# Opening of a fused attention and soft-mixture kernel: four token tiles with two heads on alternate partitions, loads on two queues

## The chip, the core and the metric

The kernel runs on one core of a Trainium2 chip. TensorE (PE) multiplies into PSUM, VectorE (DVE), ScalarE (ACT) and GpSimd (POOL) work beside it, SyncE (SP) issues loads and stores, and the DMA engines move them. The metric is device microseconds (us) of one execution; lower is better.

## The reference

Three stages follow each other. All is float32, except the first mixture's weights, which come as float64 and are narrowed on the chip.

```
# attention by chunks of 32 tokens; 4 batches, 8 heads, 768 tokens, 64 wide
q_c = q[:, :, c_start:c_end]
k_full = concat([mem_k, k[:, :, l_start:r_end]])   # 8 memory + 16 + 32 + 8 keys
a = softmax(scale * q_c @ k_full.T);  out[:, :, c_start:c_end] = a @ v_full
# a rational network on x = [3072 tokens, 512]
h = x @ w_in                                        # 2048 wide
g = (a0 + a1*h + a2*h*h + a3*h*h*h) / (1 + |b0|*|h| + |b1|*h*h + 1e-6)
x = g @ w_out
# soft mixture of 8 experts with 4 slots each
logits = x @ phi;  d = softmax(logits, over tokens);  c = softmax(logits, over slots)
slot_out[e] = relu((d.T @ x)[e] @ w1[e]) @ w2[e];  return c @ slot_out
```

## The kernel before

The 3072 tokens are six blocks of 512. A block has four tiles of 128 tokens, or two **pairs** of tiles. For a pair, `attention` multiplies queries and keys (line L168, scores), takes the largest score of each row (L186), subtracts it (L189), takes exponentials (L190), turns the result on PE so that keys lie on partitions (L208, copied out by ACT in L212), sums (L197 to L199), multiplies with the values (L228, here called **PV**), scales (L238), turns the token rows (L246) and copies them into `xt`, the block's x with features on partitions (L250). Two heads share a tensor: one has partitions 0 to 63, the other 64 to 127, and each L168 or L228 multiplies one head, one chunk of 32 tokens, over 64 partitions, so that a pair takes 64 matmuls for the scores and 64 for PV.

Then a block has eight **steps** of 256 hidden columns: `h_part` (L380, eight float32 matmuls of 512 columns in block 0, none of whose x or weights is split), ACT's Abs, Square and Identity of h (L610, L611, L613), DVE's denominator (L612) and numerator (L622, L623), ACT's Ln and Exp (L627, L628) for the reciprocal, POOL's product (L588) and two more on DVE (L635, L636). Block 0 also narrows each step's weights from float64: `f64_narrow` is a scaled copy on ACT (L303), a clamp on DVE (L304), a Prelu on ACT (L305) and a shift with or on DVE (L307). The pieces of w_in are called i0 to i7, those of the transposed w_out o0 to o7. All through block 0 the pairs of block 1 are attended to in slices between the steps.

The **opening** is what stands ahead of the first step: pair 0 (tiles A and B of the block) and pair 1 (tiles C and D), i0 to i2 narrowed, and h of step 0. Its order on PE, ACT, DVE and POOL is written out by hand: the string `pre` names generators, of which each letter advances one to its next yield (`fN` issues N dummy matmuls, L288). `loads` gives the loads in order; SP issues them all, in its own queue. Behind the opening a scheduler orders the engines from the sequence of the code (`ord0` for block 0). Each engine works through its own order strictly; SP too. Loads use eight semaphores in turn, so a load is issued only when the one eight places ahead has landed. The pools of buffers rotate: `p_g` has four (a staging buffer of 1 MB each for one i or o), `p_xt` four, `p_x` two, `ps_h` two buffers of PSUM.

Of the kernel before, what the change touches and what calls it, by code (L numbers as in the profile page):

```python
# [46 lines left out]
def tile_chunk_attention__rational__soft_moe(  # L47
# [103 lines left out]
    def attention(pair, tile4=None, after=None):  # L151
        tile4 = tile4 or (lambda shape: p_a4("a4", shape))
        after = pair + 1 if after is None else after
# [3 lines left out]
        if pair < 2:  # L157
            both = ps_h("h", [P, 2, 2, HP, WIN])
            sc = [both[:, par] for par in range(2)]
        else:  # L160
            sc = [bank([P, 2, HP, WIN]) for _ in range(2)]
# [56 lines left out]
        if pair < 2:
            both = ps_h("h", [P, 2, 2, HP, D])
            pv = [both[:, par] for par in range(2)]  # L220
        else:
            pv = [bank([P, 2, HP, D]) for _ in range(2)]
# [718 lines left out]
```

## Time and profile before

| | us |
|---|---|
| median of three runs (574.03 to 574.85) | 574.24 |
| the profiled execution, its own time | 573.23 |
| its span in the trace | 571.1 |
| PE busy | 537.9 (94%) |
| DVE busy | 455.7 (80%) |
| ACT busy | 427.8 (75%) |
| POOL busy | 122.8 (21%) |

The span is what the trace covers; 2.1 us of the profiled execution lie around it. The shares are means over stages with different limits. TensorE's granted clock is 0.984 of full speed over the span. The trace shows each float32 matmul of the attention and of block 0 as two rows, a transpose as one; "64*32 64x64" is a stationary tile of 64 partitions by 32 columns and an output of 64 columns.

### The profile page before, as it was taken

The numbers are of one execution on the slowest core, as the hardware profiler recorded it, in microseconds if no ns is written. First come the engines' busy times: TensorE is split into PE (matmuls) and PEld (weight loads), VectorE is DVE, ScalarE is ACT, GpSimd is POOL, SyncE is SP. The second block draws the span as 40 slices with busy tenths as digits, with TensorE's granted clock in tenths as the row PEclk, the third lists the DMA queues.
The fourth block names the chain that finished last, engine by engine and source line by source line (L and its number), as shares of the span: only waits on it lengthen the run. The fifth ranks groups of instructions, "written<-read, shape, count | busy, mean of one in ns | idle before, by whom it ended". The sixth has DMA issues, their size and how long they took to land.

```text
span 571.1 us, 13640 instructions
## 1 busy us (share of the span) xinstructions
PE 537.9 (94%) x5874; PEld 360.2 (63%) x5874; DVE 455.7 (80%) x572; ACT 427.8 (75%) x551; POOL 122.8 (21%) x66
## 2 busy tenths in 40 slices
PE   6799899999999999999999999999999999999981
PEld 5654445467667677677766777776778667643351
DVE  4749999999989899979799799897898978831041
ACT  1669999998978899688887887878888978721132
POOL 0001111422213132313222213132323332300000
PEclk9699999999999999999999999999999999999997
DMA  8897763313225223533233315313359264799948
GB/s 322 352 393 268 259 223 117 116 64 113 63 86 185 76 80 143 185 112 94 93 112 111 133 57 183 112 48 138 111 178 376 94 239 147 293 397 409 408 163 355
DMA packets 28139, 105.80 MB, mean 185 GB/s; under 512 B 3376, under 2 KB 3504, under 8 KB 27056
## 3 DMA queue, kind: packets, MB, share of 16 engines
q1 hardware_dynamic: 26928, 100.74, 48.4%
q0 software_dynamic: 1152, 4.19, 1.8%
q8 instruction: 46, 0.75, 0.5%
q14 instruction: 13, 0.11, 0.1%
HBM read 94.44 MB, written 10.49 MB: 184 GB/s over the span
## 4 chain that ended last, share of the span: by engine, by line
PE 47%; DVE 25%; ACT 12%; DMA 7%; issue 6%; POOL 1%; SPq 1%; ACTq 0%; DVEq 0%; POOLq 0%
PE h L380 24%; PE m L405 4%; DMA win<-in_moe_w_dram 3%; DVE T L623 3%; PE lg L398 3%; DVE T L622 3%; PE m L458 3%; DVE S L612 3%; ACT S L610 3%; DVE T L635 3%; ACT S L611 2%; DVE T L636 2%; PE m L228 2%; DVE g L304 2%; DMA T<-in_moe_w_dram 2%
## 5 line engine op out<-in xcount | busy, mean ns | idle before, releaser
L380 PE MATMUL h<-xt,win 128*128 128x512 f32 x1012 | 266.8, 412 | 1.5 <-DVE T L623 1.3
L380 PEld LDWEIGHTS h<-xt,win 128*128 128x128 f32 x1012 | 183.7, 188 | 51.0 <-issue 12.3
L588 POOL TENSOR_TENSOR S<-S,S 128x1024 f32<-128x1024 f32 x46 | 112.8, 2452 | 329.5 <-DVE S L612 329.5
L610 ACT ACTIVATE S<-h,ctab 128x1024 f32<-128x1024 f32 x47 | 52.5, 1117 | 40.3 <-PE h L380 39.5
L612 DVE SCALAR_TENSOR_TENSOR S<-S,S 128x1024 f32<-128x1024 f32 x47 | 57.3, 1218 | 28.4 <-ACT S L611 28.2
L405 PEld LDWEIGHTS m<-ident,T 128*128 128x128 f32 x384 | 43.0, 141 | 30.7 <-issue 16.2
L622 DVE TENSOR_TENSOR T<-T,h 128x1024 f32<-128x1024 f32 x47 | 56.9, 1210 | 6.2 <-ACT T L613 6.2
L623 DVE SCALAR_TENSOR_TENSOR T<-T,ctab,h 128x1024 f32<-128x1024 f32 x47 | 59.8, 1271 | 0.7
L635 DVE SCALAR_TENSOR_TENSOR T<-T,ctab,S 128x1024 f32<-128x1024 f32 x46 | 58.6, 1274 | 0.0
L406 ACT ACTIVATE g<-m 128x512 f32<-128x512 f32 x96 | 53.5, 602 | 6.5 <-PE m L405 6.3
L636 DVE SCALAR_TENSOR_TENSOR T<-S,T 128x1024 f32<-128x1024 f32 x46 | 56.1, 1220 | 2.0
L613 ACT ACTIVATE T<-h,ctab 128x1024 f32<-128x1024 f32 x47 | 57.4, 1221 | 0.0
L405 PE MATMUL m<-ident,T 128*128 128x128 f32 x384 | 53.2, 277 | 3.0 <-DVE a L189 1.4
L628 ACT ACTIVATE S<-S,ctab 128x1024 f32<-128x1024 f32 x47 | 54.4, 1158 | 0.9
L627 ACT ACTIVATE S<-S 128x1024 f32<-128x1024 f32 x47 | 50.4, 1072 | 6.1 <-DVE S L612 6.1
L611 ACT ACTIVATE S<-h,ctab 128x1024 f32<-128x1024 f32 x47 | 52.7, 1121 | 1.4 <-DVE T L635 1.4
L398 PE MATMUL lg<-T,wp 128*32 128x512 f32 x192 | 37.3, 605 | 1.3 <-DVE T L636 0.7
L380 PE MATMUL h<-xt,x 128*128 128x512 f32 x64 | 30.7, 607 | 0.0
L190 ACT ACTIVATE a<-a 128x512 f32<-128x512 f32 x22 | 13.7, 631 | 14.6 <-DVE a L189 14.6
L458 PE MATMUL m<-g,s 128*32 128x512 f32 x192 | 22.0, 595 | 0.4 <-ACT s L450 0.4
L305 ACT ACTIVATE g<-g 128x1024 f32<-128x1024 f32 x16 | 18.8, 1173 | 2.1 <-DVE g L304 2.1
L228 PE MATMUL m<-v,a 64*32 64x64 f32 x1280 | 17.6, 224 | 1.3 <-issue 0.8
(218 smaller groups left out, 661.1 us busy)
## 6 DMA issues: line engine op xcount, KB each, us to landing
win<-in_moe_w_dram SPq DMA_DIRECT2D x31, 512.0 KB, 7.7
k<-in_kw_dram SPq DMA_DIRECT2D x22, 512.0 KB, 6.3
v<-in_vw_dram SPq DMA_DIRECT2D x22, 512.0 KB, 5.3
g<-in_moe_w_in_dram SPq DMA_DIRECT2D x16, 512.0 KB, 8.1
g<-in_w_turned_dram SPq DMA_DIRECT2D x16, 512.0 KB, 5.7
x<-in_moe_w_out_dram SPq DMA_DIRECT2D x8, 1024.0 KB, 4.9
out_dram<-win SPq DMA_DIRECT2D x12, 512.0 KB, 5.0
q<-in_qw_dram SPq DMA_DIRECT2D x11, 512.0 KB, 3.7
```

The source lines that it names most:

```text
L380: PE.matmul(tile_[f2] if step == total - 1 else tile_[:, f2, :], lhsT=ww[:, c, f2 * P:f2 * P + P], rhs=xx[:, c, :], start=(n == 0), stop=( ...
L398: PE.matmul(st["lg"][32 * j:32 * j + 32, :], lhsT=wp[:, 4 * qd + j, :], rhs=gt_tile[k - 1 + j // 2][:, j % 2, :], start=(qd == 0), stop=(q ...
L405: st["turn"] = PE.transpose(pb[:, m, f2 * P:f2 * P + P], t_[:, f2, tt * P:tt * P + P], ident)
L588: POOL.tensor_tensor(out, q, w, ALU.mult)
L610: ACT.activation(s, hh, AF.Abs, scale=b0)
L611: ACT.activation(y, hh, AF.Square, scale=rb1)
L612: pins[0] = DVE.scalar_tensor_tensor(s, y, QC, s, ALU.add, ALU.add).ins
L613: pins[1] = ACT.activation(t, hh, AF.Identity, bias=a2, scale=a3).ins
L622: DVE.tensor_tensor(t, t, hh, ALU.mult)
L623: behind[kk] = DVE.scalar_tensor_tensor(t, t, a1, hh, ALU.add, ALU.mult).ins
L635: DVE.scalar_tensor_tensor(t, t, a0, w, ALU.add, ALU.mult)
L636: st["t"] = DVE.scalar_tensor_tensor(t, e, 2.0, t, ALU.subtract, ALU.mult, reverse0=True).ins
```

## The change

Block 0's attention is done by tile instead of by pair (`attention_first(n)`, n = 0 to 3 for A to D), and its two heads lie on alternate partitions: the even ones hold one head, the odd ones the other. The keys' tensor has a first free dimension for the head, and where the partition belongs to the other head it holds zeros. One matmul over 128 partitions then gives 32 tokens against both heads' windows (128 columns): 16 matmuls for a tile's scores and 16 for its PV. The zeros are filled in ahead by POOL and DVE, into buffers borrowed from the pools, and each K or V half of 256 KB is loaded into alternate partitions. Four of the loads are issued by ACT: one half each of K of tile A, K of tile B and V of tile A, and at last Q1, the queries of tiles C and D. The two coefficient loads and phi become one load (`cst`). Probabilities lie with the heads in turn in the last dimension.

h of step 0 is done in two halves (`h_first`): of tiles A and B after the second tile's x is there, of C and D at the end, 256 columns a matmul. In PE's order the last tile's PV stands between the two parts of the first half, its turn behind them. The dummy matmuls have 256 columns. Block 1's first attention slice is held behind the last matmul of `h_first`. The stack matrix takes four DVE instructions instead of 16. The lay-out of q, k and v in memory changes to suit.

```diff
 KN = {
-    'loads': "q0 q1 v0 i0 v1 c0 i1 i2 q2 o0 v2 i3".split(),
-    'pre': "f10 A A f5 B B A A A A B B A A B B A A A A s B B B B A A f2 A B B A s t A B B t A f2 B B B B c f4 u u".split(),
+    'loads': "Q0 K0 K1 V0 Q1 K2 V1 i0 K3 V2 V3 c0 i1 i2 q2 o0 v2 i3".split(),
+    'pre': "f8 A A B B A A C C B B A A A A B B C C B B s D D C C s D D C C H D D H D D c t J t J u u".split(),
...
+    def place(n):
+        k_first[n] = (p_k("k", [P, 2, HP, 4, WIN]) if n == 0 else p_xt("xt", [P, 2, HP, 4, WIN]) if n < 3 else p_x("x", [P, 2, HP, 4, WIN]))
+        v_first[n] = (p_v("v", [P, 2, 4, HP, D]) if n == 0 else p_xt("xt", [P, 2, 4, HP, D]) if n == 1 else p_x("x", [P, 2, 4, HP, D]) if n == 2 else p_g("g", [P, 2, 4, HP, D]))
+
+    def load_first(kind, n):
+        if kind == "Q":
+            q_first[n] = (p_S("S", [P, HP, 2 * P]) if n else p_q("q", [P, HP, 2 * P]))
+            (SP, ACT)[n].dma_start(out=q_first[n], in_=qw[n])
+        else:
+            t, src = (k_first[n], kw[n // 2, :, n % 2]) if kind == "K" else (v_first[n], vwin[n // 2, :, n % 2])
+            for par in range(2):
+                (ACT if par and kind + str(n) in ("K0", "K1", "V0") else SP).dma_start(out=t[par:P:2, par], in_=src[apart[par]])
+
+    def attention_first(n):
+        o = P * (n % 2)
+        sc = ps_h("h", [P, HP, 2, WIN])
+        for hp in range(HP):
+            for c in range(4):
+                PE.matmul(sc[CH * c:CH * c + CH, hp], lhsT=q_first[n // 2][:, hp, o + CH * c:o + CH * c + CH],
+                          rhs=k_first[n][:, :, hp, c, :], start=True, stop=True)
+        yield
...
+        pr = p_T("T", [P, HP, WIN, 2])
+        by = pr.rearrange("p h j a -> p h a j")
+        DVE.tensor_tensor(by, sc, mx.unsqueeze(3).to_broadcast([P, HP, 2, WIN]), ALU.subtract)
+        ACT.activation(pr, pr, AF.Exp, scale=SCALE)
+        yield
+        turned = bank([P, HP, P])
+        for hp in range(HP):
+            PE.transpose(turned[:, hp, :], pr[:, hp].rearrange("p j a -> p (j a)"), ident)
+        yield
...
+                PE.matmul(pv[CH * c:CH * c + CH, hp], lhsT=pt[:, hp, CH * c:CH * c + CH],
+                          rhs=v_first[n][:, :, c, hp, :], start=True, stop=True)
...
+    def h_first(half):
+        if 0 not in hs:
+            hs[0] = ps_h("h", [P, 2, BLK])
+        o = slice(P // 2 * half, P // 2 * half + P // 2)
+        x = xt[0][0].rearrange("p c (t r) -> p c t r", t=TT)
+        for f2 in range(2):
+            to = hs[0][:, f2, :].rearrange("p (t r) -> p t r", t=TT)
+            for c in range(NC):
+                pins["PE"] = PE.matmul(to[:, :, o], lhsT=w_f[0][:, c, f2 * P:f2 * P + P], rhs=x[:, c, :, o],
+                                       start=(c == 0), stop=(c == NC - 1)).ins
+            yield
...
+    for par in range(2):
+        (DVE, POOL)[par].memset(k_first[0][:, par], 0.0)
+    for engine, ts in ((POOL, (k_first[1], v_first[1], k_first[3], v_first[2], v_first[3])), (DVE, (v_first[0], k_first[2]))):
+        for t in ts:
+            engine.memset(t.rearrange("p a h c j -> p (a h c j)"), 0.0)
...
-        SP.dma_start(out=ctab[:, 0:4], in_=ca.unsqueeze(0).to_broadcast([P, 4]))
-        SP.dma_start(out=ctab[:, 4:6], in_=cb.unsqueeze(0).to_broadcast([P, 2]))
-        SP.dma_start(out=u_acc[:, 0:NC * NSLOT], in_=phi)
+        SP.dma_start(out=u_all[:, BLK - NC * NSLOT:BLK + 6], in_=cst)
...
-        t = ps_l("lg", [P, P])
+        t = ps_l("lg", [P, 2, P])
         for _ in range(n):
-            PE.matmul(t, lhsT=ident, rhs=ident, start=True, stop=True)
+            PE.matmul(t, lhsT=ident, rhs=ident.unsqueeze(1).to_broadcast([P, 2, P]), start=True, stop=True)
...
-    hs[0] = ps_h("h", [P, 2, BLK])
-    h_part(0, hs[0], 0)
-    h_part(0, hs[0], 1)
...
         if what == "at":
-            slice_()
+            with tc.issue_after(pins["PE"]) if kk == 0 else nullcontext():
+                slice_()
```

PE, the opening from the first dummy matmuls on, before. L288 are dummies; h holds scores and PV results, m what is turned, a and T probabilities and token rows; `x8` counts matmuls.

```order
L288 MATMUL lg_185<-ident_106 128x128 x10
L168 MATMUL h_196<-k_145,q_144 32x64 x64
L288 MATMUL lg_261<-ident_106 128x128 x5
L168 MATMUL h_267<-xt_142,xt_141 32x64 x64
L208 MATMUL m_349<-ident_106,a_1_332 128x128 x4
L208 MATMUL m_354<-ident_106,a_1_332 128x128 x4
L228 MATMUL h_373<-v_152,a_2_348 32x64 x64
...
L246 MATMUL m_564<-ident_106,T_550 128x128 x4
L288 MATMUL lg_577<-ident_106 128x128 x4
L380 MATMUL h_588<-xt_143,win_438 128x512 x8
```

The same place in the change, from the scores of tile C (L261, on keys xt_4 and queries S_1) to the last part of h (L315). L278 turns probabilities, L290 is PV, L298 turns token rows.

```order
L261 MATMUL h_3_255<-xt_4_124,S_1_154 32x128 x16
L278 MATMUL m_2_277<-ident_1_106,T_2_241 128x128 x4
L290 MATMUL h_4_288<-v_1_121,S_2_249 32x128 x16
...
L261 MATMUL h_6_353<-x_2_126,S_1_154 32x128 x16
L290 MATMUL h_7_375<-x_1_125,S_4_337 32x128 x16
L278 MATMUL m_6_395<-ident_1_106,T_4_372 128x128 x4
L298 MATMUL m_7_406<-ident_1_106,a4_3_392 128x128 x4
L315 MATMUL h_8_412<-xt_1_119,win_4_349 128x4x64 x4
L290 MATMUL h_9_417<-g_1_127,S_5_400 32x128 x16
L315 MATMUL h_8_412<-xt_1_119,win_4_349 128x4x64 x4
L298 MATMUL m_8_440<-ident_1_106,a4_4_434 128x128 x4
L315 MATMUL h_8_412<-xt_1_119,win_4_349 128x4x64 x8
```

A pair's 64 matmuls have become two groups of 16, the last tile's PV and turn stand among the parts of h, and only eight matmuls of 256 columns are left behind them. Ahead of this piece stand eight dummies, the scores of A and B, and A's turn; no dummies follow.

ACT, from the last copy into xt to the first step's activations, before (L275 to L279 prepare constants, g_168 is i2).

```order
L250 ACTIVATE xt_143<-m_564 128x16x32
L275 ACTIVATE ctab_108<-ctab_108 128x2
L278 ACTIVATE ctab_108<-ctab_108 128x1
L279 ACTIVATE ctab_108<-ctab_108 128x1
L303 ACTIVATE g_168<-g_168 128x1024
L305 ACTIVATE g_168<-g_168 128x1024
L610 ACTIVATE S_639<-h_588,ctab_108 128x1024
L611 ACTIVATE S_641<-h_588,ctab_108 128x1024
```

In the change (g_170 is i1, g_173 is i2; L371 and L373 are the two ACT parts of narrowing, L659 is Abs, L660 Square):

```order
L302 ACTIVATE xt_119<-m_440 128x16x32
L343 ACTIVATE u_109<-u_109 128x2
L346 ACTIVATE u_109<-u_109 128x1
L347 ACTIVATE u_109<-u_109 128x1
L371 ACTIVATE g_170<-g_170 128x1024
L373 ACTIVATE g_170<-g_170 128x1024
L371 ACTIVATE g_173<-g_173 128x1024
L659 ACTIVATE S_514<-h_412,u_109 128x1024
L373 ACTIVATE g_173<-g_173 128x1024
L660 ACTIVATE S_516<-h_412,u_109 128x1024
```

i1 is narrowed behind the last copy instead of between the tiles, and i2's Prelu stands between Abs and Square.

DVE, at step 1's denominator, before (g_597 is i4):

```order
L189 TENSOR_TENSOR a_4_698<-m_605,mx_700 128x8x64
L189 TENSOR_TENSOR a_4_698<-m_606,mx_719 128x8x64
L612 SCALAR_TENSOR_TENSOR S_739<-S_741,S_739 128x1024
L197 TENSOR_REDUCE sm_735<-a_4_698 128x8
L304 TENSOR_SCALAR g_597<-g_597 128x1024
L198 TENSOR_SCALAR sm_735<-sm_735 128x8
```

In the change (g_187 is i3, g_181 o0, g_472 i4; L372 and L375 are the two DVE parts of narrowing, L661 is the denominator, L671 the numerator's first product):

```order
L179 TENSOR_TENSOR a_5_573<-m_481,mx_594 128x8x64
L187 TENSOR_REDUCE sm_610<-a_5_573 128x8
L188 TENSOR_SCALAR sm_610<-sm_610 128x8
L372 TENSOR_SCALAR g_187<-g_187 128x1024
L189 RECIPROCAL sm_610<-sm_610 128x8
L375 SCALAR_TENSOR_TENSOR win_521<-g_187 128x1024
L375 SCALAR_TENSOR_TENSOR win_143<-g_181 128x1024
L661 SCALAR_TENSOR_TENSOR S_614<-S_616,S_614 128x1024
L372 TENSOR_SCALAR g_472<-g_472 128x1024
L671 TENSOR_TENSOR T_615<-T_615,h_526 128x1024
```

The sums and i3's clamp have moved ahead of step 1's denominator, and i4's clamp follows it without anything between.

## Rows read from the trace of the kernel before

**Rows 1.** Busy us of each engine, granted clock, DMA by windows: opening, block 0.

```profile
core 0: us, PE busy (x) PEld busy (x) DVE busy (x) ACT busy (x) POOL busy (x), PEclk, DMA share, GB/s
10.00:15.00 5.00, 2.30 (x131) 1.82 (x132) 2.33 (x5) 1.26 (x2) 0.00 (x0) 0.84 1.03 412
...
60.00:65.00 5.00, 3.57 (x37) 1.39 (x19) 4.95 (x8) 5.00 (x7) 0.57 (x1) 1.00 0.93 333
...
115.00:120.00 5.00, 5.00 (x26) 3.25 (x25) 5.00 (x5) 5.00 (x8) 0.00 (x0) 1.00 0.36 129
```

**Rows 2.** Timeline (start, us, instruction, idle before it): end of the opening.

```profile
30.70 7.13 PE L380 MATMUL h<-xt,win 128*128 128x512 f32 x16
...
37.87 1.11 ACT L610 ACTIVATE S<-h,ctab 128x1024 f32<-128x1024 f32 x1 [4.04 <-PE h L380]
...
40.02 1.23 DVE L612 SCALAR_TENSOR_TENSOR S<-S,S 128x1024 f32<-128x1024 f32 x1 [4.94 <-ACT S L611]
```

**Rows 3.** Timeline, PE alone, opening.

```profile
1.36 4.64 PE L288 MATMUL lg<-ident 128*128 128x128 f32 x20 [1.36 <-POOL ctab L290]
...
11.90 0.46 PE L168 MATMUL h<-xt,xt 64*32 64x64 f32 x32 [0.73 <-DMA xt<-in_kw_dram]
...
14.16 1.17 PE L168 MATMUL h<-xt,xt 64*32 64x64 f32 x64 [1.80 <-issue]
...
15.26 1.97 PE L208 MATMUL m<-ident,a 128*128 128x128 f32 x8
...
20.28 1.34 PE L228 MATMUL h<-v,a 64*32 64x64 f32 x72 [1.18 <-issue]
...
26.37 1.11 PE L228 MATMUL h<-S,T 64*32 64x64 f32 x90 [1.13 <-issue]
...
28.87 1.09 PE L246 MATMUL m<-ident,T 128*128 128x128 f32 x8 [0.35 <-DVE T L238]
```

**Rows 4.** Windows of 1 us, where the granted clock falls and rises.

```profile
13.00:14.00 1.00, 0.00 (x0) 0.00 (x0) 0.00 (x0) 0.17 (x1) 0.00 (x0) 0.72 1.03 410
...
23.00:24.00 1.00, 1.00 (x7) 0.90 (x5) 1.00 (x3) 0.74 (x2) 0.00 (x0) 0.66 1.03 418
```

**Rows 5.** Groups by line and shape: busy us, mean ns, idle before.

```profile
L458 PE MATMUL m<-g,s 128*32 128x512 f32 x192 | 22.0, 595 | 0.4 <-ACT s L450 0.4
...
L766 POOL MEMSET wp<- 128x512 f32 x1 | 0.5, 527 | 6.4 <-PE lg L398 6.4
```

**Rows 6.** Timeline, DVE and ACT instructions of the opening, one of each kind.

```profile
10.18 0.69 DVE L189 TENSOR_TENSOR a<-h,mx 128x512 f32<-128x512 f32 x1
...
10.90 0.63 ACT L190 ACTIVATE a<-a 128x512 f32<-128x512 f32 x1 [8.88 <-DVE a L189]
...
18.02 0.68 DVE L197 TENSOR_REDUCE sm<-a 128x8 f32<-128x512 f32 x1
...
20.05 0.66 DVE L304 TENSOR_SCALAR g<-g 128x1024 f32<-128x1024 f32 x1
...
20.75 1.15 ACT L305 ACTIVATE g<-g 128x1024 f32<-128x1024 f32 x1 [0.81 <-DVE g L304]
...
23.55 0.60 ACT L212 ACTIVATE T<-m 128x512 f32<-128x512 f32 x1 [0.26 <-PE m L208]
...
30.53 0.21 ACT L275 ACTIVATE ctab<-ctab 128x2 f32<-128x2 f32 x1
...
31.30 1.13 ACT L303 ACTIVATE g<-g 128x1024 uint32<-128x1024 uint32 x1
...
33.86 1.22 DVE L307 SCALAR_TENSOR_TENSOR win<-g 128x1024 uint32<-128x1024 uint32 x1 [1.21 <-ACT g L305]
```

**Rows 7.** Timeline, steps 1 and 3: DVE and POOL.

```profile
51.03 2.38 POOL L588 TENSOR_TENSOR S<-S,S 128x1024 f32<-128x1024 f32 x1 [49.68 <-DVE S L612]
...
51.40 2.56 DVE L304 TENSOR_SCALAR g<-g 128x1024 f32<-128x1024 f32 x1
...
74.82 1.19 DVE L612 SCALAR_TENSOR_TENSOR S<-S,S 128x1024 f32<-128x1024 f32 x1
```

More of the change, by code (lines that the diff above doesn't have):

```diff
@@ L149, in new_xt, with attention @@
         xt[b] = [p_xt("xt", [P, NC, BLK], F32R if b else F32) for _ in range(2 if b else 1)]
-    def attention(pair, tile4=None, after=None):
-        tile4 = tile4 or (lambda shape: p_a4("a4", shape))
-        after = pair + 1 if after is None else after
+    def attention(pair):
+        after = pair + 1
         t_first = 2 * pair
@@ L156, in attention @@
         qt, kt = ahead.pop(("q", pair))
[L157 to L161, printed above, removed]
+        sc = [bank([P, 2, HP, WIN]) for _ in range(2)]
         for n in range(2):
@@ L213, in turns @@
             yield
-        for part in (turns, sums) if pair < 2 else (sums, turns):
-            yield from part()
+        yield from sums()
+        yield from turns()
         vt = ahead.pop(("v", pair))
[L218 to L222, printed above, removed]
+        pv = [bank([P, 2, HP, D]) for _ in range(2)]
         for n in range(2):
@@ L516, in convert @@
         if n < NSTEP:
-            with tc.issue_after(pins[0]) if pins else nullcontext(), tc.issue_after(pins[1]) if pins else nullcontext():
+            with tc.issue_after(pins[0]) if 0 in pins else nullcontext(), tc.issue_after(pins[1]) if 0 in pins else nullcontext():
                 for _ in {"s": narrow_w_in, "n": narrow_w_turned, "z": wp_sum, "i": load_w_in, "o": load_w_turned}[kind](n) or ():
                     pass
-    new_xt(0)
     for what in KN["loads"]:
         load(what)
-    gens = {"A": attention(0, after=NPAIR), "B": attention(1, lambda shape: p_T("T", shape), after=NPAIR),
-            "s": narrow_w_in(0), "t": narrow_w_in(1), "u": narrow_w_in(2), "c": constants()}
+    gens = {"ABCD"[n]: attention_first(n) for n in range(4)}
+    gens.update({"H": h_first(0), "J": h_first(1), "s": narrow_w_in(0), "t": narrow_w_in(1), "u": narrow_w_in(2), "c": constants()})
     for what in KN["pre"]:
@@ L914, in _lay_out @@
     phi = np.asarray(inputs["moe2_phi"]).reshape(4, 128, 32).transpose(1, 0, 2).reshape(128, 128)
[L915 removed]
+    cst = np.concatenate([phi] + [np.tile(np.asarray(inputs[n]), (128, 1)) for n in ("moe_a", "moe_b")], axis=1)
+    return {**inputs, "cst": cst, "moe2_w2": w2, "qw": qw, "kw": kw, "vw": vw, "moe_w_in": w_in, "moe_w_out": w_out, "w_turned": w_turned}
 def kernel(**inputs):
```

115 lines of the change are left out of this document (64 added, 51 removed).

## The prediction

> **What bounds the kernel now.** I read the page's slices of the span first: TensorE is full but for the first and last ones, and the DMA is busy at the start, so the opening is a stage of its own. The windows then tell which engine is full in each stage. From 10 to 15 us PE is busy 2.30 of 5 us and DVE 2.33, while the DMA engines are full at 412 GB/s; from 60 to 65 DVE has 4.95, ACT 5.00 and PE only 3.57; from 115 to 120 all three have 5.00 [rows 1]. So block 0 is bound by DVE and ACT, and time won ahead of it is time won at the end, if both engines get their work earlier by as much. The timeline gives the mark to measure by: h of step 0 takes 7.13 us on PE from 30.70, ACT has waited 4.04 us for it when Abs starts at 37.87, and DVE has waited 4.94 us when step 0's denominator starts at 40.02 [rows 2]. From there to step 3's denominator at 74.82 [rows 7] are 34.8 us.
>
> PE alone shows what the opening spends. The scores of pair 1 begin a second half at 14.16 after 1.80 us without a releaser, PV waits 1.18 us in the same way at 20.28 and 1.13 at 26.37, and between are 126 to 128 matmul rows each time, 6.1 us apart: the supply of instructions, I take it, which small matmuls use up [rows 3]. That is 4.1 us. And the granted clock falls from full to half in 13 to 14 us, after that stretch of 2.30 busy us in 5, and rises in 23 to 24, with PE busy without a pause since 20.28 [rows 1, 3, 4]; eight transposes took 1.97 us at the lower level and 1.09 at the higher [rows 3].
>
> **The loads.** The change moves the same bytes in another order. Before, six loads of 0.524 MB had landed at 11.90, where PE waits for the sixth [rows 3]. In the change the scores of tile C need Q1 and K2; in order of issue up to these stand Q0, K0, the constants, V0, K1, half of V1, K2 and Q1, 3.48 MB, 0.33 more. At 0.412 MB a us that is 0.8 us later: **12.7**. Bounds: 13.9 if the rest of V1 and a quarter of i0 (0.26 MB each) go first, and 12.1 if ACT's queue, which holds only Q1 by then, gets every second turn and its half megabyte doesn't wait for what SP has queued. How two queues share the engines no row shows. [...]
>
> Zeros: 512 columns took POOL 0.527 us [rows 5], so 2048 take at most 2.1 and 1024 1.05; POOL's six end at 1.3 + 11.6 = 12.9, and DVE's three, at the same rate, at about 6. Nothing else is due on either: DVE's first scores come at 8.4, POOL's first product at 51.03 [rows 7]. I cost them at nothing. If they took twice as long, V3, and i1, i2 and the third q behind it on SP, would be issued at 24 instead; V3 would then land at about its use at 26 to 27, the others ahead of theirs.
>
> The eight dummies are as many columns as 16 of before, of which 10 took 4.64 us [rows 3]; at the lower clock they would end at 8.8, with a rise at 6 near 7.2. Q0 and K0, 1.05 MB, land at about 6.8 at the rate of the loads above, and the scores of A are 4 us off the path that counts.
>
> **PE's pieces.** No row has a 32-column stationary tile with 128 columns moving. The bound from below is the 64 rows of 1.17 us at the low clock [rows 3], half of that for 32 rows, 0.6. From above: 192 rows of 512 columns took 22.0 us, 0.115 each [rows 5], a quarter of that for 128 columns, 32 times: 0.92. The second is the same tile shape, so 0.9 at the full clock and 1.7 at the low one, and 0.2 us until the last result is there. Four transposes are 0.65 or 1.0 [rows 3]; a quarter of h, four matmuls of 256 columns, 1.78 (7.13 / 4) [rows 2]. Tiles C and D take 128 rows in over 8 us, more than the 6.1 in which before got as many, so I count no wait for instructions.
>
> **The chain.** From 12.7 I follow the four orders by hand, each instruction after the one ahead of it and after what it reads, with 0.69 for a reduce, subtract or multiply of 512 columns, 1.1 for sums with their two small followers (0.68 and 0.4), 0.63 for an exponential, 0.60 for a copy, 1.13, 0.66, 1.15 and 1.22 for the four parts of narrowing [rows 6]. For the clock I take the low level from 13.4 to 17.4, a shorter time than before since PE has work without pause from 12.7 to 16.7.
> C's scores are done at 14.0, reduced and subtracted at 15.4, B's sums at 16.4; PE has done B's turn and A's PV by 16.7. A's multiply 17.4, turn 18.1, B's PV 19.0, multiply 19.7. Then DVE: C's sums 20.8, i0's clamp 21.4, D's reduce and subtract 22.7. ACT does i0's Prelu until 23.2, D's exponential until 23.7. PE: D's turn 24.4, C's turn 24.9, a quarter of h, D's PV 27.5, a quarter of h and D's turn 29.7 (multiplied meanwhile), ACT's copy 30.3, the last half of h **34.0**. Before, h ended at 37.8, so PE gains 3.8. ACT doesn't: behind that copy stand the constants (0.77, from 30.53 to 31.30 [rows 6]), i1's two parts and i2's first, until 34.6. Abs follows at 34.5, i2's Prelu, then Square until 37.7, and DVE's denominator starts at **37.9**, 2.1 us ahead of 40.02 [rows 2].
>
> Bounds: clock never falling 37.3; low until 20.8, 39.2; loads at 12.1 give 37.3, at 13.9 39.4.
>
> **Steps 0 to 3.** Followed in the same way with the orders of block 0, step 3's denominator starts 35.3 us after step 0's, against 34.8. In step 1 ACT waits 0.7 us for the first subtract of the next pair and DVE 1.6 us for i3's Prelu; against that, i4's clamp, which took 2.56 us instead of 0.66 while POOL multiplied [rows 6, 7], now starts right behind the denominator, ahead of POOL; i5's clamp loses 0.4 to POOL in step 2. Cost 0.5, bounds 0 (both orders equal) and 2.4 (i4's clamp blocked all the same, 1.9 more). Behind step 3 the orders read alike.
>
> **Sum.** -2.1 + 0.5 = -1.6: 571.6 for the profiled execution (573.23, its span 571.1 and 2.1 around it). The median of the runs is 574.24, 1.0 above, so **572.6**, 0.28% less. A measurement of this kernel tells about 0.2%, 1.15 us, from nothing.
>
> **Rivals.**
> (a) Both bounds on the good side: loads at 12.1, the clock never low, no loss in steps 0 to 3. The chain then ends at 36.6, a gain of 3.4: 570.8. For it: the 412 GB/s on one queue [rows 1], which leave the queues to share. Against: PE idles between A's turn (11.4) and 12.7, much as it did before the clock fell [rows 4].
> (b) The opening is shorter, and nothing of it arrives: ACT's narrowing behind the copy, a load at 13.9 and a clock low until near 20 put the denominator at 39.3, and steps 0 to 3 take the rest: 574.0. For it: DVE and ACT are full in block 0 [rows 1], so that every instruction moved from the opening into it is paid there.
> [...]
> (d) Slower: loads of 64 rows on every second partition move at less than the full rate. At 0.3 MB a us Q1 and K2 land near 16, the denominator starts at 41.8: +1.8 + 0.5, 576.5. The gain is gone below 0.36 MB a us. No row has such a load.
>
> **Chances.** The forecast (gain 1.2 to 2.6) 0.40, (a) 0.17, (b) 0.24, (c) 0.09, (d) 0.10. Faster by over 0.2%: 0.57; within: 0.24; slower: 0.19. The range goes from 570.0, below (a) by a quarter of its gain, to 576.5, (d); that leaves out (c) and a little at both ends. The likeliest case's own range is 571.6 to 573.0.
>
> **What would show it.** In the profile after: C's scores (L261 on S) begin at 12 to 14; no PE wait "issue" over 1 us between 12 and 30; the granted clock back at full before 21; the last half of h ends at 33 to 36; Abs (L659) at 34 to 36; the first L661 at 37 to 39.5; the fourth L661 at 72 to 75. The forecast is wrong if C's scores start after 15, if the last L302 copy ends after 32, or if the first and the fourth L661 gain by different amounts, more than 2 us apart.

## The result and the profile after

The change made the kernel slower: 578.86 us (median of five runs, 576.22 to 580.96) against 574.03, a ratio of 1.0086 (95% interval 1.006 to 1.0112). The forecast was 572.6 with a range to 576.5. The profiled execution took 580.52, 8.9 more than the 571.6 of the forecast's sum, and its span is 578.7.

I measure as the prediction did, by the start of DVE's denominator of a step (L661, L612 before; step 46 is the last one with such a line). This is after less before:

| denominator of step | 0 | 1 | 2 | 3 | 13 | 15 | 46 | end of the span |
|---|---|---|---|---|---|---|---|---|
| us later than before | +1.5 | +4.2 | -0.2 | +5.8 | +8.4 | +6.7 | +6.7 | +7.6 |

So there are four pieces. The opening is 3.6 worse than forecast (+1.5 for -2.1); steps 0 to 3 take 39.1 us for the forecast 35.3; steps 3 to 15 lose 0.9, and so does the end. That is 9.2; 0.3 comes back because 1.8 us lie around this span instead of 2.1. Between steps 15 and 46 the difference stays.

The windows of the changed kernel show both places: busy time of PE, its weight loads, DVE, ACT and POOL with their instructions, then the granted clock, the DMA engines' share and GB/s.

```profile
5.00:10.00 5.00, 3.33 (x41) 2.41 (x39) 2.83 (x8) 0.00 (x0) 5.00 (x4) 1.00 0.86 287
10.00:15.00 5.00, 2.21 (x36) 1.56 (x36) 2.60 (x5) 1.23 (x3) 0.98 (x2) 0.76 0.96 350
60.00:65.00 5.00, 4.82 (x136) 2.40 (x134) 4.88 (x7) 5.00 (x7) 0.81 (x1) 1.00 1.01 381
65.00:70.00 5.00, 2.22 (x10) 0.92 (x11) 5.00 (x5) 3.93 (x5) 1.55 (x1) 0.72 0.58 202
70.00:75.00 5.00, 5.00 (x15) 2.65 (x14) 5.00 (x5) 1.86 (x4) 0.00 (x0) 0.59 0.99 378
...
12.00:13.00 1.00, 1.00 (x33) 0.72 (x24) 0.05 (x1) 0.00 (x0) 0.00 (x0) 0.81 1.01 381
20.00:21.00 1.00, 0.39 (x4) 0.39 (x4) 0.56 (x1) 0.00 (x0) 0.00 (x0) 1.00 1.03 393
67.00:68.00 1.00, 0.22 (x4) 0.23 (x8) 1.00 (x2) 0.88 (x1) 0.00 (x0) 0.61 0.06 25
```

From 10 to 15 us the DMA moves 350 GB/s where it moved 412 [rows 1], and from 5 to 10 us 287, where the kernel before has 392 (its own row is below). From 65 to 70 PE has 2.22 busy us of 5, after 4.82 in the five before, and the granted clock is at half (0.50) from 67.2 to 74.1. In the opening it is at half from 12.6 to 19.4.

**The opening.** This is the timeline of the changed kernel from its start to step 0's denominator: zero fills, SP's loads, C's scores on PE, then the last copy on ACT and the denominator on DVE. A row that holds several instructions gives the start of the first and the length of all; the bracket is the engine's wait and what ended it.

```profile
2.14 3.55 POOL L334 MEMSET xt<- 128x2048 f32 x2
2.31 1.76 DVE L334 MEMSET v<- 128x2048 f32 x1 [0.38 <-issue]
...
1.96 0.55 SPq L254 DMA_DIRECT2D k<-in_kw_dram  x1
2.56 0.57 SPq L340 DMA_DIRECT2D u<-in_cst_dram  x1
4.10 0.48 SPq L254 DMA_DIRECT2D v<-in_vw_dram  x1
4.62 0.77 SPq L254 DMA_DIRECT2D xt<-in_kw_dram  x1
7.96 2.98 SPq L254 DMA_DIRECT2D xt<-in_kw_dram  x2
...
15.15 1.93 PE L261 MATMUL h<-xt,S 128*32 128x128 f32 x32 [1.20 <-DMA xt<-in_kw_dram]
33.49 0.60 ACT L302 ACTIVATE xt<-m 128x512 f32<-128x512 f32 x1 [4.67 <-PE m L298]
41.54 1.22 DVE L661 SCALAR_TENSOR_TENSOR S<-S,S 128x1024 f32<-128x1024 f32 x1
```

K0's halves are issued at 1.96 (SP) and 2.24 (ACT), and the next load of keys or values only at 3.98 (a half of K1, by ACT, behind POOL's first fill). V0 by SP goes out at 4.10, behind DVE's fill of v (2.31 to 4.07), and K1's other half behind V0 at 4.62. The constants' small load, twelfth in the code, has moved to third place in SP's order, since only PE, ACT, DVE and POOL keep the hand's order there. Of K2, the first half waits until 7.96 for the semaphore that the constants' load, eight places ahead, holds; the second goes out at about 10.5 (within the row's 2.98 us), behind V0's landing. The waits of SP's queue up to 35 us say the same of K2 (in total, times and longest):

```profile
SPq L254 <- DMA v<-in_vw_dram: 2.0, 1, 2.0
SPq L254 <- DMA u<-in_cst_dram: 1.7, 1, 1.7
```

Q1, which C's scores need too, goes out by ACT at 7.49 and lands 6.3 us later, ahead of K2's second half. So C's scores start at 15.15 instead of 12.7, and everything behind follows, 26.4 us to the denominator.

**Step 2.** The timeline of the changed kernel from step 2's denominator to step 3's, DVE, ACT, POOL and PE:

```profile
62.83 1.22 DVE L661 SCALAR_TENSOR_TENSOR S<-S,S 128x1024 f32<-128x1024 f32 x1
63.56 1.18 ACT L373 ACTIVATE g<-g 128x1024 f32<-128x1024 f32 x1
64.19 2.37 POOL L636 TENSOR_TENSOR S<-S,S 128x1024 f32<-128x1024 f32 x1 [6.28 <-issue]
64.77 2.86 DVE L375 SCALAR_TENSOR_TENSOR win<-g 128x1024 uint32<-128x1024 uint32 x1
67.78 1.08 PE L551 MATMUL m<-win,u 128*32 128x256 f32 x8 [2.96 <-DVE win L375]
68.80 3.78 PE L448 MATMUL h<-xt,win 128*128 128x512 f32 x4
80.65 1.22 DVE L661 SCALAR_TENSOR_TENSOR S<-S,S 128x1024 f32<-128x1024 f32 x1
```

The narrowing of o1 (clamp L372, Prelu L373, shift L375) comes late. Its clamp ends just as the denominator is due, ACT's Prelu runs beside that, POOL starts the product that the denominator frees, and the shift, which starts 0.58 us behind it, takes 2.86 us instead of 1.22. PE's matmuls of o1 with phi (L551) stand ahead of the next h in PE's order, and PE waits 2.96 us. Then the clock is at half, and four rows of h, that is two matmuls, take 3.78 us (1.98 at the full clock, at 58.63). In the kernel before the same shift stood ahead of step 2's denominator and took 1.22 us; PE waited 1.43 us for it, as its timeline shows:

```profile
61.33 1.22 DVE L307 SCALAR_TENSOR_TENSOR win<-g 128x1024 uint32<-128x1024 uint32 x1
62.70 0.64 PE L483 MATMUL m<-win,u 128*32 128x256 f32 x8 [1.43 <-DVE win L307]
63.07 1.21 DVE L612 SCALAR_TENSOR_TENSOR S<-S,S 128x1024 f32<-128x1024 f32 x1
```

The shift's 2.86 us end 1.07 after POOL's product does (66.56); the next shift, at 71.08 with POOL idle, took 1.21. That the product delays the shift is read from this, and what holds it no run shows.

**Steps 3 to 15.** PE's busy time from step 3's denominator to step 15's is the same (121.66 us before, 121.32 after), and the stretch is 124.65 and 125.52 long. PE's longest waits in this stretch of the changed kernel (80.65 to 206.17), in total, times and longest:

```profile
PE m L473 <- ACT g L474: 2.2, 2, 1.2
PE m L484 <- ACT s L482: 1.5, 1, 1.5
```

In the kernel before (74.82 to 199.47) the first kind is 0.7 us, the second isn't there, and two waits of 1.0 and 0.8 have no releaser. DVE's order from step 3 to step 17 differs from before's in three places, and ACT's, for which PE waits here, in more.

### The profile page after: what moved, and what is told of

It reads as the page before. It is cut to its first block, busy times and chain, and to the rows that moved or that the text cites. A ratio compares the mean times of both kernels' runs of the same rounds, so it can differ in the third digit from the quotient of the medians.

```text
span 578.7 us, 13117 instructions
## 1 busy us (share of the span) xinstructions
PE 540.2 (93%) x5604; PEld 360.7 (62%) x5604; DVE 459.3 (79%) x562; ACT 427.8 (74%) x551; POOL 132.4 (23%) x72
## 4 chain that ended last, share of the span: by engine, by line
PE 62%; ACT 15%; DVE 13%; DMA 4%; issue 3%; POOL 1%; SPq 0%; ACTq 0%; DVEq 0%; POOLq 0%
PE h L448 31%; PE m L473 5%; PE lg L466 4%; PE m L526 4%; ACT S L659 3%; ACT S L660 3%; ACT g L474 3%; PE m L214 3%; PE h L851 2%; DMA v<-in_vw_dram 2%; PE lg L888 2%; DVE T L671 2%; DVE T L672 2%; PE m L232 2%; PE m L198 1%
## 5 line engine op out<-in xcount | busy, mean ns | idle before, releaser
L448 PE MATMUL h<-xt,win 128*128 128x512 f32 x996 | 260.9, 411 | 2.4 <-DVE T L672 2.2
L448 PEld LDWEIGHTS h<-xt,win 128*128 128x128 f32 x996 | 181.7, 189 | 50.3 <-issue 10.9
L659 ACT ACTIVATE S<-h,u 128x1024 f32<-128x1024 f32 x47 | 52.4, 1114 | 35.8 <-PE h L448 35.1
L661 DVE SCALAR_TENSOR_TENSOR S<-S,S 128x1024 f32<-128x1024 f32 x47 | 57.3, 1220 | 22.5 <-ACT S L660 22.2
L671 DVE TENSOR_TENSOR T<-T,h 128x1024 f32<-128x1024 f32 x47 | 57.0, 1212 | 6.7 <-ACT T L662 6.7
L672 DVE SCALAR_TENSOR_TENSOR T<-T,u,h 128x1024 f32<-128x1024 f32 x47 | 59.8, 1273 | 0.7
L684 DVE SCALAR_TENSOR_TENSOR T<-T,u,S 128x1024 f32<-128x1024 f32 x46 | 58.6, 1274 | 0.0
L662 ACT ACTIVATE T<-h,u 128x1024 f32<-128x1024 f32 x47 | 57.3, 1220 | 0.0
L677 ACT ACTIVATE S<-S,u 128x1024 f32<-128x1024 f32 x47 | 54.3, 1156 | 0.9
L660 ACT ACTIVATE S<-h,u 128x1024 f32<-128x1024 f32 x47 | 52.6, 1118 | 0.9 <-DVE T L684 0.9
L375 DVE SCALAR_TENSOR_TENSOR win<-g 128x1024 uint32<-128x1024 uint32 x12 | 16.2, 1357 | 5.8 <-ACT g L373 5.7
L373 ACT ACTIVATE g<-g 128x1024 f32<-128x1024 f32 x16 | 18.4, 1152 | 0.2 <-DVE g L372 0.2
L371 ACT ACTIVATE g<-g 128x1024 uint32<-128x1024 uint32 x16 | 18.6, 1169 | 0.0
```

What stands on the lines that cost most here:

```text
L448: PE.matmul(tile_[f2] if step == total - 1 else tile_[:, f2, :], lhsT=ww[:, c, f2 * P:f2 * P + P], rhs=xx[:, c, :], start=(n == 0), stop=( ...
L659: ACT.activation(s, hh, AF.Abs, scale=b0)
L660: ACT.activation(y, hh, AF.Square, scale=rb1)
L661: pins[0] = DVE.scalar_tensor_tensor(s, y, QC, s, ALU.add, ALU.add).ins
L662: pins[1] = ACT.activation(t, hh, AF.Identity, bias=a2, scale=a3).ins
L671: DVE.tensor_tensor(t, t, hh, ALU.mult)
```

## The experiments

The theory after this: (A) the loss is in the orders of steps 1 and 2 and in late loads of the opening, each of which can be mended alone, and the attention by tile itself does what was forecast. The rivals: (B) alternate partitions load slowly (the prediction's case d); (C) the cost is the clock, which falls in the opening and in step 2, and the orders matter only through it; (D) the attention by tile is itself longer than forecast. The texts put in below letter their theories each for itself: theory C in them is a load's wait for the one eight places ahead, rival D the zero fills or the second queue, and rival B of the first text the opening's own delay.

**Order of step 2.** The changed kernel with three pins: in the sequence of step 1 the narrowing of o1 (`n0`) ahead of step 0's last two products on DVE (`t`), these two products behind o1's clamp, step 2's denominator behind its shift.

```diff
+            with tc.issue_after(st["shift"]) if kk == 2 else nullcontext():
                 pins[0] = DVE.scalar_tensor_tensor(s, y, QC, s, ALU.add, ALU.add).ins
...
-                with tc.issue_after(behind[kk]) if kk in behind else nullcontext():
+                with tc.issue_after(behind[kk]) if kk in behind else nullcontext(), tc.issue_after(st["clamp"]) if kk == 1 else nullcontext():
...
+            if kk == 1:
+                steps = [w for w in steps if w != "n0"]
+                steps.insert(steps.index("t"), "n0")
```

> The change with one place of block 0 put back as it stood before: o1's clamp ahead of step 0's two last products on DVE, o1's shift ahead of step 2's denominator. Theory A (the time is lost where the matmuls of wp_sum for o1 wait 2.96 us for that shift, behind POOL's product, and the clock falls at 67.3): the wait shrinks to 1.5 us or less, no fall between 50 and 100 us, step 3's denominator starts at 75.5 to 77.5 instead of 80.65, and the median comes to 573.5 to 575.5. Rival B (the opening's own delay is the loss and the rest of block 0 only carries it): step 3's denominator moves by less than 2 us and the median stays at 577 or more.

Measured: 574.28 (572.65 to 575.29), 1.0005 times before (0.9991 to 1.002). Its timeline:

```profile
41.70 1.22 DVE L662 SCALAR_TENSOR_TENSOR S<-S,S 128x1024 f32<-128x1024 f32 x1
...
64.84 1.22 DVE L662 SCALAR_TENSOR_TENSOR S<-S,S 128x1024 f32<-128x1024 f32 x1
64.85 0.64 PE L551 MATMUL m<-win,u 128*32 128x256 f32 x8
76.97 1.22 DVE L662 SCALAR_TENSOR_TENSOR S<-S,S 128x1024 f32<-128x1024 f32 x1
```

PE's matmuls of o1 no longer wait, and steps 0 to 3 take 35.27 us (41.70 to 76.97), which is the forecast 35.3. (A)'s time and its mark hold; that the clock would stay up does not, it was low from 59 to 63 after a wait of 1.59 at 58.83. The scheduler's order of blocks 0 and 1 moved too: from step 3 to step 15 this kernel gains 1.3 on the kernel before, with 1.75 us of idle PE (before 2.99, after 4.20). So the 4.6 us between the two medians are the pins and what the scheduler made of them, not the one wait alone.

**Cover for the clock.** The changed kernel with seven dummy matmuls of 256 columns ahead of the matmuls that wait, meant to keep PE busy while it would wait.

```diff
+        if i == 1:
+            cover = ps_l("lg", [P, 2 * P])
+            for _ in range(7):
+                last_cover = PE.matmul(cover, lhsT=ident, rhs=gt_tile[0][:, 0, 0:2 * P], start=True, stop=True).ins
+            pin = tc.issue_after(last_cover)
...
+        with pin:
```

> The change with seven dummy matmuls of 256 columns (3.0 us) on PE ahead of wp_sum for o1, which fill the wait and push three matmuls of h behind it. Nothing of the late shift is mended; only the clock is kept up. If the fall of the clock from 67.3 to 74.0 us costs 3.3 us of the 5.8 that step 2 loses, the median comes to 575 to 577 and the runs lie within 2 us of each other, where those of the change lay 4.7 apart. If the wait itself is the cost and the clock none, the time stays at 578 to 581.

Measured: 577.25 (575.79 to 579.97), 1.0059 (1.0035 to 1.0083), and the wait is there still. Its timeline and its windows:

```profile
63.88 1.22 DVE L668 SCALAR_TENSOR_TENSOR S<-S,S 128x1024 f32<-128x1024 f32 x1
68.84 0.64 PE L558 MATMUL m<-win,u 128*32 128x256 f32 x8 [2.14 <-DVE win L375]
78.88 1.23 DVE L668 SCALAR_TENSOR_TENSOR S<-S,S 128x1024 f32<-128x1024 f32 x1 [0.26 <-ACT S L667]
```

```profile
65.00:70.00 5.00, 2.86 (x18) 1.66 (x18) 4.89 (x5) 4.35 (x6) 2.38 (x1) 1.00 0.69 262
70.00:75.00 5.00, 5.00 (x19) 2.71 (x18) 5.00 (x6) 2.83 (x4) 0.00 (x0) 1.00 0.95 347
```

The clock is 1.00 in every window from 24 to 125 us. Steps 0 to 2 take 21.3 as in the changed kernel, step 2 to 3 takes 15.0 instead of 17.8: the clock was at least 2.8 of the 3.8 us that steps 0 to 3 lose to the forecast, the order by itself at most 1.0, since the dummies also push three matmuls of h behind the wait. The median is just above what was expected, and the runs lie 4.2 us apart where at most 2 were expected. In the profiled execution (578.67) the clock was low in the opening, from 17 to 24, and the denominator of step 0 came at 42.58.

**A control.** The text below is written for loads of 64 rows, but the kernel that ran has no such edit: it is the kernel before once more.

> The kernel before, with each K and V load of the opening cut in two by partitions (0 to 63, 64 to 127): loads of 0.26 MB and 64 rows as in the change, one queue, no zero fills. Theory C (a load waits for the one eight places ahead, so that half as large loads leave half as many bytes under way): the rate from 5 to 10 us falls from 392 to 340 GB/s or less, and the second pair's scores, which wait for the DMA, start at 12.7 or later instead of 11.90. Rival D (the zero fills or the second queue slow the loads of the change): 380 GB/s or more, scores at 11.7 to 12.3.

Measured: 573.85 against 573.74, 1.0003 (0.9988 to 1.0018). It tells nothing of 64 rows, and shows how well two times of one kernel agree.

**SP in the written order.** The changed kernel, with SP too held to the hand's order in the opening, so that the constants' load is no longer third.

```diff
-    start.enter_context(tc.manual_schedule(engines={e.engine for e in (PE, ACT, DVE, POOL)}))
+    start.enter_context(tc.manual_schedule(engines={e.engine for e in (PE, ACT, DVE, POOL, SP)}))
```

> The change with SP's queue in the order of the string loads: the constants' load behind V3 instead of third, V0's half behind K1's, K2 ahead of V1, so that K2 waits for Q0 and a half of K0 instead of for the constants and V0. Theory C: tile C's scores start at 12.7 to 14.2 instead of 15.15, and step 0's denominator 1 us or more earlier than 41.54. Rival (loads of alternate partitions are slow in themselves): 15 or later. The order of block 0 changes with it: step 2 reads otherwise, so its time is read apart from the opening's.

Measured: 579.05 (578.02 to 580.92), 1.0094 (1.0068 to 1.0121). C's scores come 0.4 earlier only, and block 0's order, which the scheduler makes again, has other waits on PE, here at 60.31:

```profile
14.76 1.08 PE L261 MATMUL h<-xt,S 128*32 128x128 f32 x32 [2.10 <-DMA xt<-in_kw_dram]
...
39.97 1.22 DVE L661 SCALAR_TENSOR_TENSOR S<-S,S 128x1024 f32<-128x1024 f32 x1
60.31 1.26 PE L448 MATMUL h<-xt,win 128*128 128x512 f32 x2 [3.89 <-DVE T L672]
77.15 1.21 DVE L661 SCALAR_TENSOR_TENSOR S<-S,S 128x1024 f32<-128x1024 f32 x1
```

For C's scores neither side's number holds. K2 is now issued from 6.24 on instead of from 7.96, and that is worth only 0.4: the DMA still moves 231 GB/s from 2.5 to 5 us and 255 from 5 to 10. Step 0's denominator comes 1.6 us earlier, at 39.97, 25.2 behind C's scores. Steps 0 to 3 take 37.2 (the changed kernel 39.1), with the clock low from 61 to 65, and steps 3 to 15 take 127.3 (125.5), with a mean clock of 0.66 from 105 to 110. The profiled execution, 579.18, is 1.3 shorter than that of the changed kernel, and the two medians don't differ: this run wins nothing that its median shows.

**Loads of half the partitions, in the kernel before.** The K and V loads of its opening in two pieces each: partitions 0 to 63 and 64 to 127, or even and odd. Both for (B), one run each.

```diff
-            SP.dma_start(out=tk[:, o], in_=kw[pair, :, o])
+            for r in (slice(0, 64), slice(64, 128)) if pair < 2 else (slice(0, 128),):
+                SP.dma_start(out=tk[r, o], in_=kw[pair, r, o])
```

(and `(slice(0, 128, 2), slice(1, 128, 2))` in the other; V alike.)

> The kernel before, with each K and V load of the opening cut in two by partitions, 0 to 63 and 64 to 127: loads of 0.26 MB and 64 rows, one queue, no zero fills (e3 was meant to be this, but was built without the edit and so ran the kernel before as it is). Theory C (the load eight places ahead must have landed, so smaller loads leave fewer bytes under way): from 5 to 10 us 340 GB/s or less instead of 392, the second pair's scores first wait until 12.7 or later instead of 11.90. Rival D (the zero fills, or the second queue): 380 GB/s or more, scores at 11.4 to 12.3.

> The same cut by even and odd partitions. If alternate partitions are slower in themselves, the rate with the DMA engines fully busy is lower than in the run cut into halves, near the 345 GB/s that the change shows for K3, V2 and V3 (15 to 20 us), and the second pair's scores come later still, by 0.5 us or more. If only the size of a load matters, both runs read alike within 0.3 us.

Measured: 581.15 with the halves, 576.45 with even and odd, against 573.97. The windows, first those of the kernel before, then with even and odd, then with halves:

```profile
5.00:10.00 5.00, 3.40 (x140) 2.88 (x140) 0.66 (x2) 0.00 (x0) 0.00 (x0) 1.00 0.97 392
```

```profile
5.00:10.00 5.00, 3.50 (x140) 3.01 (x140) 0.52 (x2) 0.00 (x0) 0.00 (x0) 1.00 0.95 320
10.00:15.00 5.00, 1.52 (x75) 1.07 (x75) 2.47 (x5) 1.26 (x2) 0.00 (x0) 0.83 1.02 406
```

```profile
5.00:10.00 5.00, 2.61 (x55) 1.66 (x62) 0.00 (x0) 0.00 (x0) 0.00 (x0) 1.00 1.00 257
10.00:15.00 5.00, 4.36 (x137) 3.81 (x131) 2.99 (x6) 0.88 (x2) 0.00 (x0) 1.00 1.04 231
```

Even and odd rows move 320 GB/s from 5 to 10 us, where whole loads move 392, and 406 from 10 to 15; pair 1's scores come at 12.73, 0.8 later than before [rows 3]. So alternate partitions in loads of half the size cost 0.8 us, not the 3.3 at 0.3 MB a us that case d had. Which part of the 0.8 is the smaller load and which the alternation, these two don't tell: neither reading of the second text came, since halves are the slower cut by far (scores at 16.06). Nor is the full rate there all the time, 320 GB/s being moved with the DMA engines 0.95 busy. What lets (B) fall as the cause is the run of the loads alone, below: all its K and V loads go to alternate partitions, and C's scores start at 12.80.

**Loads and orders anew.** The changed kernel with SP in order, other places for the loads (K2's zeros ahead of V0's, V3 in V0's buffer), and pins for i4, i5 and o1.

```diff
-    'loads': "Q0 K0 K1 V0 Q1 K2 V1 i0 K3 V2 V3 c0 i1 i2 q2 o0 v2 i3".split(),
+    'loads': "Q0 K0 K1 Q1 K2 V0 V1 i0 K3 V2 c0".split(),
+    'pre': "f8 A A B B A A C C B B A +V3 +i1 +i2 A A A B B C C B B s D D C C s D D C C H D +q2 +o0 D H D D +v2 +i3 c t J t J u u".split(),
...
+    for engine, ts in ((POOL, (k_first[1], v_first[1], k_first[3], v_first[2])), (DVE, (k_first[2], v_first[0]))):
```

(A letter behind a + issues that load at its place.)

> The change with both suspected losses mended. Loads: SP in written order, K2 right behind K1 and its zeros filled ahead of V0's, so that no load up to K2 waits for one eight places ahead; the constants behind K3 and V2; V3 into V0's buffer. Block 0: i4's and o1's narrowing on DVE placed as in the kernel before. Theory (these two are the whole loss, and the chain from tile C's scores to step 0's denominator is 25.2 us): C's scores at 12.0 to 13.2, step 0's denominator at 37.2 to 38.6, step 3's at 72.5 to 74.5, median 571.5 to 573.5. Rival (a gain ahead of block 0 is taken back there because DVE and ACT are full): step 3's denominator at 75 or later and the median at 574 or more.

Measured: 575.42 (574.4 to 577.55), 1.0028 (1.0016 to 1.004). The theory's numbers are missed and the rival's two are met (step 3's denominator at 75.57), but by the timeline for a new reason, ahead of block 0:

```profile
14.30 1.08 PE L262 MATMUL h<-xt,S 128*32 128x128 f32 x32 [1.54 <-DMA S<-in_qw_dram]
```

Q1, issued by ACT at 4.51, took 9.7 us to land while SP's loads went on. Steps 0 to 3 took 35.6.

**Q1 by SP, second; orders as in the first experiment.** To its three pins come: Q1 issued by SP right behind Q0, K2's zeros ahead of V0's on DVE, the V loads issued behind K2.

```diff
-    'loads': "Q0 K0 K1 V0 Q1 K2 V1 i0 K3 V2 V3 c0 i1 i2 q2 o0 v2 i3".split(),
+    'loads': "Q0 Q1 K0 K1 K2 V0 V1 i0 K3 V2 V3 c0 i1 i2 q2 o0 v2 i3".split(),
...
-            (SP, ACT)[n].dma_start(out=q_first[n], in_=qw[n])
+            SP.dma_start(out=q_first[n], in_=qw[n])
...
-    for engine, ts in ((POOL, (k_first[1], v_first[1], k_first[3], v_first[2], v_first[3])), (DVE, (v_first[0], k_first[2]))):
+    for engine, ts in ((POOL, (k_first[1], v_first[1], k_first[3], v_first[2], v_first[3])), (DVE, (k_first[2], v_first[0]))):
...
-        load(what)
+        with tc.issue_after(st["K2"]) if "K2" in st and what[0] == "V" else nullcontext():
+            load(what)
```

> The run e1 with one thing more: Q1 is loaded by SP, second, while the zeros of K0, K1 and K2 are filled in (K2's ahead of V0's), and V0 and V1 are issued behind K2. All orders of PE, ACT, DVE and POOL are those of e1, so only the loads differ. Theory (the opening of the change is late by its loads alone: SP waits for zero fills and for loads eight places ahead while the DMA engines run dry, and from tile C's scores on the chain takes 25 to 26 us): C's scores at 10.8 to 12.8 instead of 15.7, step 0's denominator at 36.5 to 38.6 instead of 41.70, step 3's at 72 to 74 instead of 76.97, and the median at 570.5 to 572.5, below both kernels. Rival (b) of the prediction (what is won ahead of block 0 is paid back in it, since DVE and ACT are full there): step 3's denominator moves by less than half as much as step 0's and the median stays at 573.5 or more.

Measured: 571.58 (571.41 to 572.93), 0.9957 times before (0.9939 to 0.9975): faster than both kernels. Its timeline:

```profile
1.18 0.42 SPq L250 DMA_DIRECT2D S<-in_qw_dram  x1
...
13.06 1.08 PE L263 MATMUL h<-xt,S 128*32 128x128 f32 x32
38.74 1.23 DVE L665 SCALAR_TENSOR_TENSOR S<-S,S 128x1024 f32<-128x1024 f32 x1
73.65 1.22 DVE L665 SCALAR_TENSOR_TENSOR S<-S,S 128x1024 f32<-128x1024 f32 x1
```

The load stands in the time in which the loads of K1 wait for their zeros: 380 GB/s from 2.5 to 5 us, 239 in the changed kernel. C's scores wait for no load. They and step 0's denominator come 0.3 and 0.1 later than the text's bounds; step 3's denominator and the median hold, and rival (b) doesn't. Steps 0 to 3 take 34.9, and the denominator of step 0 is 1.3 ahead of before. The rest of the gain isn't the forecast's: 1.4 us come from steps 3 to 15, as in the first experiment, and 1.0 is lost at the end.

**The same, on the loads and orders anew.** Q1 by SP in the second place, in the kernel of the last experiment but one.

> The run e6 with the same edit of the loads (Q1 by SP, second); all else as in e6, where C's scores waited until 14.30 for Q1, which ACT had issued at 4.51. Theory: C's scores at 10.8 to 12.5, step 0's denominator at 36.5 to 38.5 instead of 39.95, step 3's 2 us or more earlier than 75.57, median 572.5 to 574. If Q1 on ACT's queue was not what was late (the bytes ahead of it were), C's scores come at 13.5 or later.

Measured: 573.85 (572.37 to 575.55), 0.999 (0.9973 to 1.0007). The median holds, the places don't: C's scores start at 13.52, 0.8 earlier than in that kernel but in the range of the text's rival, step 0's denominator at 39.22, step 3's at 74.64. Yet C's scores wait for no load: B's had waited for K1 until 10.89, and the clock was low from 11 to 15. The median is 1.6 lower than in that kernel.

**The loads alone.** The changed kernel with the four edits of the loads and without the three pins.

> The change with the loads of e7 alone; block 0's orders are those of the change, o1's shift behind step 2's denominator. If the two losses are separate, step 0's denominator starts at 37.5 to 39.5 as in e7, steps 0 to 3 take 38 to 40 us as in the change (39.1) because o1's shift still stands behind POOL's product, and the median lies 2 to 3.5 us below that of the change and 3.5 to 5.5 above that of e7: 575 to 577. If the late shift only mattered because the opening was late, steps 0 to 3 take 36 us or less and the median is that of e7.

Measured: 575.89 (574.83 to 577.85), 1.0032 (1.0017 to 1.0046). Its timeline:

```profile
12.80 1.08 PE L263 MATMUL h<-xt,S 128*32 128x128 f32 x32
37.93 1.22 DVE L664 SCALAR_TENSOR_TENSOR S<-S,S 128x1024 f32<-128x1024 f32 x1
64.19 1.08 PE L553 MATMUL m<-win,u 128*32 128x256 f32 x8 [2.97 <-DVE win L377]
77.00 1.22 DVE L664 SCALAR_TENSOR_TENSOR S<-S,S 128x1024 f32<-128x1024 f32 x1
```

The opening is the forecast's to a tenth (C's scores 12.7, denominator 37.9), though with the clock full at C's scores (1.08 us; 1.93 at half clock in the changed kernel), and step 2 loses what it lost in the changed kernel: a wait of 2.97, the clock at half behind it (the eight rows of L553 in 1.08 us; 0.64 in the first experiment), 39.07 us for steps 0 to 3. The two causes are apart, and they add up. The pins are worth 4.3 us here (575.89 to 571.58) and 4.6 in the changed kernel (578.86 to 574.28); the loads 3.0 without the pins and 2.7 with them. So (A) holds, (C) is part of it, in step 2, and of (D) no more than about half a microsecond is left, which the chain in the next section shows.

**The changed kernel again**, beside it on the same chip.

> The change itself once more, beside the run before and on the same chip, for its spread and for the place where the clock falls: median 577.5 to 580; from run to run it moves by 3 us or more where e7's runs lay within 1.5. In the profile PE waits about 3 us for o1's shift near 65 us in any case; whether the clock falls there decides 3 us.

Measured: 579.06 (575.58 to 581.79), 1.0083 (1.0058 to 1.0108), with the wait of 2.97 us at 68.58 and the clock low from 13 to 20 and 68 to 75. Over its runs the time follows the mean granted clock: 575.58 and 576.54 are runs at 0.99, the four of 580.78 and above are at 0.979 to 0.98. That spread is why this kernel's interval is wide.

## Why the prediction was wrong

**The loads: the step that failed first.** "At 0.412 MB a us that is 0.8 us later: 12.7", with 13.9 as the bound. C's scores came at 15.15. The step counted bytes in a full queue. The queue was not full: loads waited for their zeros until 3.98 to 4.62, and for a semaphore eight places ahead until 7.96 and about 10.5. The step had the constants' load in its place, third, but not the semaphore that it holds. The lower bound of 12.1 fell with it: ACT's queue did not hold only Q1, but halves of K1 and V0 too, issued at 3.98 and 4.51, and Q1 landed at 13.8. "I cost them at nothing", said of the zero fills, failed with it: the fills were hidden on POOL and DVE, and not for the loads behind them. Mending only the loads gives 12.80 and 37.93, and from C's scores to the denominator 25.1 us, where the forecast had 25.2; with SP in order it is 25.2, in the fastest kernel 25.7. That these agree so well is in part luck. My 25.2 held a clock low from 13.4 to 17.4, and in all three kernels C's scores took 1.08 us, as at the full clock (1.00 from 10 to 20 us with SP in order and in the fastest); my bound for that case, 37.3, is 24.6 behind 12.7, so the pieces take 0.5 to 1.1 longer than I added up. In the changed kernel the clock was low from 12.6 to 19.4, and the chain took 26.4: of the 3.6 us that the opening lost to the forecast the loads are 2.4 and the chain 1.2. One thing of this step did come as forecast: none of the three waits without a releaser, 4.1 us in the kernel before [rows 3], is left on PE between 12 and 30 us. That they were the supply of instructions was my reading of the rows. The trace before has a transfer of 16 KB in an instruction queue, 1.0 to 1.1 us long, from 11.78, 17.90 and 24.01, each of which ends 1.3 to 1.4 us ahead of the end of such a wait; more of the cause no run shows.

**Steps 0 to 3: the step that failed second.** 35.3 forecast, bounds 34.8 and 37.2; 39.1 measured. The step looked at i4's and i5's clamps and left out o1's shift, which the new order puts behind a denominator and POOL's product. What that costs is 3.8 us, at least 2.8 of them the clock. With the order mended the size is right (35.27 and 34.9).

**"Behind step 3 the orders read alike."** They don't quite: 0.9 us go between steps 3 and 15, where PE's longest waits for ACT are 3.7 us in all, and were 0.7 before. Another 0.9 goes at the end, of which the forecast had nothing.

**The rivals.** (b), 574.0, had the right place for part of the loss, block 0's full DVE and ACT; it gave 1.4 us to the opening and block 0 together, and steps 0 to 3 alone lost 3.8. (c), a clock low through the opening until 31, didn't come: it is back at full at 19.4. It fell once more in step 2, where I had no clock on the account at all. (d) gave a time near the result by a cause that the runs refute; its condition, alternate rows at less than the full rate, holds only in part (320 GB/s, then 406), and with the loads' order mended C's scores came at 12.80 on the same alternate rows. The statement of what would make the forecast wrong named all three marks that were then seen: scores after 15, the last L302 copy ending at 34.09, the first and fourth L661 4.3 us apart.

**Open.** Why the scheduler places o1's narrowing later stays open; its order of block 0 changes with where the constants' load stands. Why the clock stayed up after one wait of 1.6 us of PE (58.63 in the changed kernel) and not after another (58.83 in the first experiment) the rows don't tell. And the last twelve stores: from the first one's issue to the end of the span they take 18.1 us in all four profiles of the kernel before and its variants, and 19.2 to 20.0 in eight of nine profiles of the changed kernel and its variants (18.2 with the cover). In the changed kernel that is 1.4 us more; 0.5 is won ahead of the first store, which leaves the 0.9 at the end. No run tells the reason.

## What to carry to other kernels

Before a transfer is costed by its bytes, ask when it can be issued: who writes its buffer first (here zero fills, which the loads awaited until 3.98 to 4.62), which load eight places ahead holds its semaphore (here the constants', until 7.96), and whether the engine that issues it keeps the order that the code has. When work ahead of a scheduled stage changes, read again every instruction that a full engine waits for there, not only those the change names: here one shift of 1.2 us, behind POOL, cost 3.8 with the clock that fell. Two losses in one change are told apart by mending each alone and both together; here the mended whole is 0.4% faster than the kernel before, and the change as made 0.9% slower. And look where a gain arises: here about half of it comes from an order behind step 3 that only the pins brought.

## What the runs showed of the hardware that was not expected

Loads to partitions 0 to 63 and 64 to 127 in turn moved 231 to 257 GB/s with all DMA engines busy (share 1.00 and 1.04); even and odd partitions, as many bytes in as many loads, 320 and then 406 (0.95 and 1.02). What sets the two apart no run shows.

A wait of PE of 3 us in a stage where it had been busy 4.82 of 5 us was followed by 6.9 us at half clock (67.2 to 74.1). With seven dummy matmuls ahead and 2.14 us of the wait left, the clock stayed at full, and step 2 to 3 took 2.8 us less.
